# Other layouts for x, the MLP's units and the weight loads of a two-layer decode kernel

## The chip, the core and the metric

The kernel runs on one core of a Trainium2 chip (trn2). The metric is the device time of one execution in microseconds. The kernel before took 519.84, 520.56 and 521.16 us in three runs: a median of 520.56. One more execution was profiled; every duration below that is not called a median comes from it.

## The reference

One token passes through two identical layers. Each layer is an attention block A and an MLP block B, with a residual around each:

```
x = A_x                                         # [1, 1, 640]
twice:
    x = x + A(layernorm(x))
    x = x + B(layernorm(x))

A(x):  q = x @ wq                               # 640 -> 32 heads of 192
       scores of q against the last 4096 keys of each head's cache, softmax, times the values
       return heads @ wo                        # 6144 -> 640
B(x):  h  = gelu(layernorm(x) @ w1)             # shifted along a sequence of length 1:
       x1 = x + 0                               # the shifts push all of h out
       return x1 + gelu(layernorm(x1) @ w3) @ w4   # 640 -> 1536 -> 640
```

Both layers use the same cache and the same weights. All inputs are bf16. Each head's K and V window is 4096 x 192, 1536 KB each.

## The kernel before

**What is kept where.** x is held as a column tile [128, 5]: 640 = 5 x 128. Element `n*128 + p` sits in partition p, column n. The MLP's 1536 units are held as [128, 12]. wq stays in SBUF for the whole kernel (`wq_sb`). A tile `wx_sb` holds the ends of w3 and w4, so that layer 1 reads only the parts that go into cells. Eleven cells of 12 KB a partition take everything else: K and V of one head each, a chunk of wo, w3, w4, transposed K kept from layer 0 for layer 1 (seven heads).

**The order of the loads.** `stream` is a list of all loads, written out by hand: wq and x first, then K and V of the heads with chunks of wo between them, then w3 and w4, and the same for layer 1. SP issues them in this order, up to eight in flight; `take` gives a load the cell that was freed longest ago, so that a load can wait for a cell. Every load is spread over 128 partitions and so over the sixteen DMA engines, eight partitions an engine; a run of contiguous bytes in a partition is a packet.

**Attention** works on groups of four heads. DVE transposes K (L377), PE multiplies it by the spread query (L453), softmax runs across PE, DVE and ACT (L478 to L537), and PE multiplies the probabilities by V (L569). DVE's L576 and PE's L583 fold the result into a column `oT`. A group's part of the product with wo goes one of two ways: `out_proj` (L597) loads a 128x128 block of wo as weights and moves one column through it, 30 blocks a group; `out_row` (L615) loads `oT` as the weights and moves wo's rows through, 2 x 320 columns for each of six chunks, into two rows of an accumulator that `turn_row` (L637) turns into a column afterwards. `out_row` serves four or five middle groups of a layer, `out_proj` the others.

**The mixer** (block B) takes the centred x as `xc`, multiplies it by w3 in 60 blocks of 128x128 (L901, into two halves of six columns each), computes gelu on ACT and DVE (L907 to L920), and multiplies by w4 in 60 blocks (L933). L938 (layer 1) or L940 (layer 0) adds the residual. In layer 0 the next layer's attention follows: mean (L325), q (L407), spread query (L421 to L436), scores. The cells of w3 and w4 are free for the next K and V after L901 and L933.

**Two places where the layout shows.** The unit that w3's block `fc` computes must be the unit that w4's block `fc` expects. w4 is read in pairs of rows (2560 B a run), so w3's columns are taken with a step of two:

```
f0 = 2 * P * (fc // 2) + fc % 2
... lhsT=w3[kc][:, f0:f0 + 2 * P - 1:2], rhs=xc[:, kc:kc + 1]
... y2_ps[:, n:n + 1], lhsT=w4[fc][:, n * P:(n + 1) * P], rhs=hT[:, fc:fc + 1]
```

And x is read as five rows of 128 (L127), cast to f32 (L313) and transposed on PE (L316); the result is transposed back on PE (L954), copied by DVE (L956) and stored as five rows of 256 B (L957).

**Loads in packets.** wq: five loads of 12288 B a partition. w3 in layer 0: two loads, five packets of 3072 B a partition; in layer 1: two loads of two such packets. w4 in layer 0: four loads, five packets of 2560 B and two of 1280; in layer 1: three loads, four of 2560 and one of 1280.

Of the kernel before, what the change touches and what calls it, by code (L numbers as in the profile page):

```python
# [9 lines left out]
F32 = mybir.dt.float32  # L10
# [7 lines left out]
P = 128  # L18
# [17 lines left out]
def kernel(  # L36
# [14 lines left out]
    nc = tc.nc  # L51
# [30 lines left out]
    assert NA * D + FREE - 2 * VW <= FREE  # L82

    W3C, W4C = FREE // F, FREE // D
    assert W4C % 2 == 1 and W4C < NF
# [38 lines left out]
    def load_x():  # L124

        x_bf = wx_sb[0:ND, 4 * P:5 * P]
        nc.sync.dma_start(x_bf, A_x.rearrange("a b (n p) -> (a b n) p", p=P))  # L127
        return x_bf
# [27 lines left out]

    def load_wq(layer, kc):
        nc.sync.dma_start(wq_sb[:, kc, :], A_wq[kc * P:(kc + 1) * P, :])
        return wq_sb
# [192 lines left out]
    def row_space(layer):  # L352

        t, i = ((wx_sb, 8 * P), (kx, 0))[layer]
        return t[0:33, i:i + D].bitcast(F32), t[0:33, i + D:i + D + QC // 2]

    kept = {}
    area = [None, 0]
# [23 lines left out]
    def qproj_steps(c, xc, part=None, row=None):  # L382
# [6 lines left out]
        def project():  # L389
            need("wq", 0, ND - 1)  # L390
            if row is not None:
# [199 lines left out]
    def out_proj(layer, *terms):  # L591

        y_ps = psm.tile([P, ND], F32, tag="psm")
        order = [(c, oT, n, k) for c, oT in terms for k in range(NA) for n in range(ND)]
        for i, (c, oT, n, k) in enumerate(order):
            wo_t = need("wo", layer, c)
            nc.tensor.matmul(  # L597
                y_ps[:, n:n + 1], lhsT=wo_t[:, k * D + n * P:k * D + (n + 1) * P], rhs=oT[:, k:k + 1],
                start=(i == 0), stop=(i == len(order) - 1))
        for c, _ in terms:  # L600
            if (layer, c) == (0, 0):
                loaded["wo", 1, 0] = wo_t
                cell_of["wo", 1, 0] = cell_of.pop(("wo", 0, 0))
            else:
                give(("wo", layer, c))
        return y_ps

    def out_row(layer, c, oT, acc, first):

        wo_t = need("wo", layer, c)  # L610
        N = D // 2
        yr_ps = psm.tile([33, N], F32, tag="psm")
        for k in range(NA):
            for i in range(2):
                nc.tensor.matmul(yr_ps[32 * i:32 * i + 1, :], lhsT=oT[:, k:k + 1],  # L615
                                 rhs=wo_t[:, k * D + i * N:k * D + (i + 1) * N], start=(k == 0), stop=(k == NA - 1))
        give(("wo", layer, c))

        def add():
            for i in range(2):  # L620
                r = slice(32 * i, 32 * i + 1)
                if first:
                    nc.vector.tensor_copy(acc[r, :], yr_ps[r, :])
                else:
                    nc.vector.tensor_add(acc[r, :], acc[r, :], yr_ps[r, :])

        return add

    def turn_row(acc):
        y_ps = psm.tile([P, ND], F32, tag="psm")  # L630
        N = D // 2
        for n in range(ND):
            a, b = n * P, (n + 1) * P
            for i in range(2):
                lo_, hi = max(a, i * N), min(b, (i + 1) * N)
                if lo_ < hi:
                    nc.tensor.matmul(y_ps[lo_ - a:hi - a, n:n + 1], lhsT=acc[:, lo_ - i * N:hi - i * N],  # L637
                                     rhs=ident[0:33, 32 * i:32 * i + 1], start=True, stop=True)
        return y_ps
# [220 lines left out]
    def mixer(layer, x_cur, z, rs_cur, ss_cur, x_new, rs_new):  # L860
# [33 lines left out]
        for ks in kcs:  # L894
            for half, hp in enumerate(h_ps):
                order = ([(i, kc) for kc in ks for i in range(HF)] if ks is kcs[0] else
                         [(i, kc) for i in range(HF) for kc in ks])
                for j, (i, kc) in enumerate(order):
                    fc = half * HF + i
                    f0 = 2 * P * (fc // 2) + fc % 2  # L900
                    nc.tensor.matmul(  # L901
                        hp[:, i:i + 1], lhsT=w3[kc][:, f0:f0 + 2 * P - 1:2], rhs=xc[:, kc:kc + 1],
                        start=(ks is kcs[0] and j == 0), stop=(ks is kcs[-1] and j == len(order) - 1))
# [28 lines left out]
        for i, (n, fc) in enumerate(order):  # L932
            nc.tensor.matmul(  # L933
                y2_ps[:, n:n + 1], lhsT=w4[fc][:, n * P:(n + 1) * P], rhs=hT[:, fc:fc + 1],
                start=(i == 0), stop=(i == len(order) - 1))
# [16 lines left out]

    row_ps = psm.tile([ND, P], out.dtype, tag="psm")
    nc.tensor.transpose(row_ps[:, :], x4[:, :], Eq[:].rearrange("p j b -> p (j b)"))  # L954
    o_fin = Lb[0:ND, :]
    nc.vector.tensor_copy(o_fin, row_ps[:])  # L956
    nc.sync.dma_start(out.rearrange("a b (n p) -> (a b n) p", p=P), o_fin)  # L957

# [29 lines left out]
```

## Time and profile before

| what | value |
|---|---|
| median of three runs | 520.56 us |
| profiled execution: its time | 519.84 us |
| profiled execution: its span | 518.0 us |
| granted TensorE clock, mean | 0.70 |
| PE, DVE, ACT busy | 63%, 57%, 10% |
| bytes read | 216.47 MB, 418 GB/s over the span |
| chain that ended last | DMA 50%, PE 23%, DVE 22% |

The page cuts the span into 40 slices of 13 us. It also has the time of the DMA packets as a share of sixteen engines' span: one queue, SP's, has nearly all of it. The time from issue to landing (part 6 of the page) tells how deep the queue is: 26.3 us for a K load whose bytes take under 4 us to move. Where that is short, 6.2 us for the first load of wq and 7.4 for the shortest V load, little was queued ahead. The chain that ended last is followed back from the last instruction; a DMA piece on it means that the next step waited for that landing, from its issue on. The trace also has every packet, with its size and duration, and for every load one landing mark from each DMA engine; a load has landed with the last of its marks.

PE's group durations are those of one matmul from start to end. Matmuls are pipelined, so where many follow each other their starts tell the pace: for L901 and L933 27 ns from one to the next.

### The profile page before, as it was taken

What the parts mean: (1) busy time and instruction counts of PE and PEld (TensorE: products, weight loads), DVE (VectorE), ACT (ScalarE), POOL (GpSimd) and SP (SyncE); (2) the same over time, 40 slices, a digit from 0 to 9 for tenths busy, and PEclk for the clock granted to TensorE, in tenths of its full rate; (3) what the DMA queues carried; (4) which work ended last, traced back from release to release, by engine and by line L of the source; (5) the groups of instructions that cost most, each with busy time, mean ns of one, the idle gap of its engine ahead of it and who ended that gap; (6) DMA issues with size and microseconds to landing.
All of it is one profiled execution on the core that took longest, in us unless ns stands there. A gap on an engine that the chain in (4) does not pass through costs nothing.

```text
span 518.0 us, 9589 instructions
## 1 busy us (share of the span) xinstructions
PE 324.8 (63%) x4146; PEld 192.6 (37%) x4146; DVE 295.2 (57%) x589; ACT 49.5 (10%) x175; POOL 4.0 (1%) x16
## 2 busy tenths in 40 slices
PE   2057656666664566767755866777566856648665
PEld 2024334333332334434333634434333433425334
DVE  2067667575584655656624356567675765664722
ACT  1000101010010100001011111001010101001011
POOL 2000000000000000000000000000000000000000
PEclk9999878565586755677665778557785676776855
DMA  8999999999999999999999999999999999999995
GB/s 347 433 425 426 433 426 427 432 428 425 433 426 427 431 426 429 428 426 431 424 425 396 385 426 429 428 428 428 429 426 427 432 428 426 426 434 426 427 416 235
DMA packets 23949, 217.08 MB, mean 419 GB/s; under 512 B 2532, under 2 KB 3044, under 8 KB 8420
## 3 DMA queue, kind: packets, MB, share of 16 engines
q1 hardware_dynamic: 23908, 216.48, 99.0%
q8 instruction: 32, 0.52, 0.4%
q14 instruction: 9, 0.07, 0.0%
HBM read 216.47 MB, written 0.00 MB: 418 GB/s over the span
## 4 chain that ended last, share of the span: by engine, by line
DMA 50%; PE 23%; DVE 22%; issue 2%; ACT 1%; SPq 1%; DVEq 0%; ACTq 0%
DMA cell<-in_A_k_cache_dram 39%; DVE cell L377 16%; DMA cell<-in_A_v_cache_dram 9%; PE ST_ps L453 9%; PE O_ps L569 7%; DVE o_sb L576 2%; DMA cell<-in_B_w_dram 2%; DVE pm L478 1%; PE nb_ps L501 1%; DVE o_sb L512 1%; ACT o_sb L507 1%; PE y_ps L637 1%; PE l_ps L528 1%; PE PT_ps L523 1%; PE qT_ps L407 1%
## 5 line engine op out<-in xcount | busy, mean ns | idle before, releaser
L453 PE MATMUL ST_ps<-cell,Qblk 128*16 128x256 bf16 x1536 | 163.7, 380 | 106.9 <-DVE cell L377 69.4
L377 DVE STREAM_TRANSPOSE cell<-cell 128x768 uint32<-128x768 uint32 x228 | 204.1, 945 | 15.2 <-DMA cell<-in_A_k_cache_dram 14.9
L453 PEld LDWEIGHTS <-Qblk 128*16 128x16 bf16 x1536 | 86.1, 111 | 176.5 <-issue 150.3
L569 PE MATMUL O_ps<-cell,PT 128*2 128x384 bf16 x1018 | 99.9, 461 | 8.2 <-DMA cell<-in_A_v_cache_dram 7.4
L576 DVE STREAM_TRANSPOSE o_sb<-O_ps 128x384 f32<-128x384 f32 x64 | 37.2, 581 | 111.8 <-PE O_ps L569 111.6
L569 PEld LDWEIGHTS <-PT 128*2 128x2 bf16 x1024 | 46.0, 100 | 22.1 <-issue 10.1
L512 DVE STREAM_TRANSPOSE o_sb<-o_sb 128x256 bf16<-128x256 bf16 x16 | 7.1, 446 | 33.2 <-ACT o_sb L507 24.2
L584 ACT ACTIVATE oT<-oT_ps,rl 32x6 bf16<-32x6 f32 x40 | 10.3, 258 | 164.0 <-PE oT_ps L583 157.8
L583 PEld LDWEIGHTS oT_ps<-o_sb,Lq 128*32 128x32 f32 x160 | 13.3, 145 | 19.3 <-issue 15.8
L583 PE MATMUL oT_ps<-o_sb,Lq 128*32 128x6 f32 x160 | 13.9, 195 | 10.4 <-DVE o_sb L576 9.9
L589 ACT ACTIVATE oT<-oT_ps,rl 32x6 bf16<-32x6 f32 x24 | 6.2, 258 | 107.6 <-PE ST_ps L453 87.1
L407 PE MATMUL qT_ps<-xc,wq_sb 128*128 128x1 bf16 x210 | 7.1, 165 | 12.8 <-DMA wq_sb<-in_A_wq_dram 12.0
L523 PE MATMUL PT_ps<-o_sb,Eq 128*32 128x32 bf16 x256 | 7.3, 237 | 9.3 <-DVE o_sb L512 4.1
L523 PEld LDWEIGHTS <-Eq 128*32 128x32 bf16 x256 | 5.4, 108 | 19.8 <-issue 19.7
L421 DVE TENSOR_TENSOR Xq<-qT_ps,maskq 128x24 bf16<-128x24 f32 (+1 forms) x18 | 2.8, 158 | 17.1 <-PE qT_ps L407 17.1
L396 PE MATMUL qr_ps<-wq_sb,xc 128*1 128x384 bf16 x90 | 12.1, 415 | 0.0
L407 PEld LDWEIGHTS <-wq_sb 128*128 128x128 bf16 x210 | 6.7, 102 | 14.0 <-DMA wq_sb<-in_A_wq_dram 13.0
L504 ACT COPY nb_sb<-nb_ps 128x1 f32<-128x1 f32 x16 | 2.5, 159 | 94.6 <-PE nb_ps L501 94.6
L615 PE MATMUL yr_ps<-cell,oT 128*1 128x320 bf16 x108 | 11.2, 355 | 0.0
L528 PE MATMUL l_ps<-lh,ones 128*128 128x4 f32 x32 | 7.7, 310 | 4.9 <-ACT PT L526 4.9
L428 PE MATMUL Qrep_ps<-Xq,Lb 128*128 128x24 bf16 (+1 forms) x18 | 3.2, 178 | 11.1 <-DVE Xq L421 10.8
L588 PE MATMUL oT_ps<-o,Lq 128*32 128x6 f32 x48 | 6.1, 199 | 6.5 <-DVE o L587 6.5
(143 smaller groups left out, 200.9 us busy)
## 6 DMA issues: line engine op xcount, KB each, us to landing
cell<-in_A_k_cache_dram SPq DMA_DIRECT2D x57, 1536.0 KB, 26.3
cell<-in_A_v_cache_dram SPq DMA_DIRECT2D x57, 1536.0 KB, 25.8
cell<-in_A_wo_dram SPq DMA_DIRECT2D x13, 960.0 KB, 26.5
wq_sb<-in_A_wq_dram SPq DMA_DIRECT2D x5, 1536.0 KB, 12.2
cell<-in_A_v_cache_dram SPq DMA_DIRECT2D x4, 768.0 KB, 23.8
cell<-in_A_v_cache_dram SPq DMA_DIRECT2D x2, 1248.0 KB, 11.5
cell<-in_B_w_dram SPq DMA_DIRECT2D x1, 1536.0 KB, 11.9
cell<-in_B_w_dram SPq DMA_DIRECT2D x2, 768.0 KB, 10.3
```

Source lines behind the costliest of these rows:

```text
L377: nc.vector.transpose(Tu, Ku[:, :, q * NY:(q + 1) * NY])
L396: nc.tensor.matmul(qr_ps[32 * i:32 * i + 1, :], lhsT=xc[:, kc:kc + 1], rhs=wq_sb[:, kc, t0 * P + i * N:t0 * P + (i + 1) * N], start=(kc == ...
L407: nc.tensor.matmul(qT_ps[:, tl:tl + 1], lhsT=wq_sb[:, kc, t * P:(t + 1) * P], rhs=xc[:, kc:kc + 1], start=(kc == 0), stop=(kc == ND - 1))
L453: nc.tensor.matmul(ST_ps[r:r + QW, :].rearrange("p (g i) -> p g i", g=ng), lhsT=Q[:, n, :], rhs=T4[:, :, f, :, t], start=(hq == 0 and n == ...
L512: nc.vector.transpose(held["PrT"], held["Pr"])
L523: nc.tensor.matmul(PT_ps[32 * m:32 * (m + 1), :, :, ng * q:ng * (q + 1)], lhsT=Eq[:, q, :], rhs=src[:, m:QW:NM], start=True, stop=True)
L528: nc.tensor.matmul(l_ps[:], lhsT=ones[:], rhs=held["lh"][:], start=True, stop=True)
L569: nc.tensor.matmul(O_ps[r:r + 2, :], lhsT=PT[:, hq, 2 * i:2 * i + 2], rhs=v_pair(V, h, 2 * i * Dh, 2 * Dh), start=(i < 4), stop=(i >= NB - 4))
L576: nc.vector.transpose(o_sb[:], O_ps.rearrange("p (e a c) -> p e c a", e=2, c=NA))
L583: nc.tensor.matmul(oT_ps[r, :], lhsT=Lq[:], rhs=o_sb[:, e, :, e], start=(e == 0), stop=(e == 1))
L584: nc.scalar.activation(oT[r, :], oT_ps[r, :], ACTF.Copy, scale=rl[r, 0:1])
L615: nc.tensor.matmul(yr_ps[32 * i:32 * i + 1, :], lhsT=oT[:, k:k + 1], rhs=wo_t[:, k * D + i * N:k * D + (i + 1) * N], start=(k == 0), stop= ...
```

## The change

x goes 5 elements to a partition: element `5*p + n` sits in partition p, column n. The MLP's units go 12 to a partition. So rows 5p to 5p+4 of wq and w3, and rows 12p to 12p+11 of w4, belong to partition p, and lie next to each other in memory.

- wq is read in two loads of 24576 and 36864 B a partition, one packet each.
- w3 is read as one packet of 12288 B (layer 0: and one of 3072 B; layer 1: two of 6144 B). w4: 11520 and 3840 B in layer 0, and 5120, 5120 and 1280 B in layer 1.
- The blocks of weights are read in steps: w3's columns with a step of 12 elements (24 B, before 2 elements), w4's and wo's with a step of 5 (10 B, before 1).
- `out_row` moves wo in steps of 5, 384 columns into one row and 256 into the other; `turn_row` takes five blocks of 128 from them.
- x is read as one row of 1280 B and spread by five matmuls with one row of weights each; the cast and the transpose go.
- The result is stored from the [128, 5] tile, 10 B a partition; the transpose and the copy before the store go.

```diff
+    WQ_PARTS = (0, 2), (2, ND)
...
-        x_bf = wx_sb[0:ND, 4 * P:5 * P]
-        nc.sync.dma_start(x_bf, A_x.rearrange("a b (n p) -> (a b n) p", p=P))
+        x_bf = wx_sb[0:1, 2 * P:2 * P + D]
+        nc.sync.dma_start(x_bf, A_x.rearrange("a b d -> (a b) d"))
...
-    def load_wq(layer, kc):
-        nc.sync.dma_start(wq_sb[:, kc, :], A_wq[kc * P:(kc + 1) * P, :])
+    def load_wq(layer, i):
+        a, b = WQ_PARTS[i]
+        nc.sync.dma_start(wq_sb[:, a:b, :].rearrange("p c n -> p (c n)"),
+                          A_wq.rearrange("(p c) n -> p (c n)", c=ND)[:, a * HD:b * HD])
...
-        src = B_w3.rearrange("(k p) f -> p k f", p=P)
+        src = B_w3.rearrange("(p k) f -> p (k f)", k=ND)
         n = W3C if layer == 0 else W3C // 2
         for k in range(0, W3C, n):
-            nc.sync.dma_start(t[:, k * F:(k + n) * F].rearrange("p (k f) -> p k f", f=F), src[:, k:k + n, :])
+            nc.sync.dma_start(t[:, k * F:(k + n) * F], src[:, k * F:(k + n) * F])
         if layer == 0:
-            nc.sync.dma_start(wx_sb[:, 0:(ND - W3C) * F].rearrange("p (k f) -> p k f", f=F), src[:, W3C:, :])
+            nc.sync.dma_start(wx_sb[:, 0:(ND - W3C) * F], src[:, W3C * F:])
...
-        pairs = B_w4.rearrange("(k p two) n -> p k (two n)", p=P, two=2)
-        ones_ = B_w4.rearrange("(k p two) n -> p k two n", p=P, two=2)
-        h = W4C // 2
-        n = h if layer == 0 else h // 2
-        for k in range(0, h, n):
-            nc.sync.dma_start(t[:, 2 * k * D:2 * (k + n) * D].rearrange("p (k n) -> p k n", k=n), pairs[:, k:k + n, :])
-        nc.sync.dma_start(blocks[2 * h], ones_[:, h, 0, :])
+        src = B_w4.rearrange("(p k) n -> p (k n)", k=NF)
+        h = W4C - 1
+        cuts = [0, W4C] if layer == 0 else [0, h // 2, h, W4C]
+        for a, b in zip(cuts, cuts[1:]):
+            nc.sync.dma_start(t[:, a * D:b * D], src[:, a * D:b * D])
         if layer == 0:
-            nc.sync.dma_start(blocks[2 * h + 1], ones_[:, h, 1, :])
-            rest = NF // 2 - h - 1
-            nc.sync.dma_start(wx_sb[:, x0 + D:x0 + D + 2 * rest * D].rearrange("p (k n) -> p k n", k=rest),
-                              pairs[:, h + 1:, :])
+            nc.sync.dma_start(wx_sb[:, x0:x0 + (NF - W4C) * D], src[:, W4C * D:])
...
-    stream = [("wq", 0, 0), ("x",)] + [("wq", 0, kc) for kc in range(1, ND)] + layer_stream(0) + layer_stream(1)
+    stream = [("wq", 0, 0), ("x",), ("wq", 0, 1)] + layer_stream(0) + layer_stream(1)
...
-    x_rf = wx_sb[0:ND, 6 * P:8 * P].bitcast(F32)
-    nc.vector.tensor_copy(x_rf, x_bf)
...
-    nc.tensor.transpose(xT_ps[:, :], x_rf, ident[0:ND, 0:ND])
+    for n in range(ND):
+        nc.tensor.matmul(xT_ps[:, n:n + 1], lhsT=x_bf[:, n::ND], rhs=Eq[0:1, 0, 0:1], start=True, stop=True)
...
-                y_ps[:, n:n + 1], lhsT=wo_t[:, k * D + n * P:k * D + (n + 1) * P], rhs=oT[:, k:k + 1],
+                y_ps[:, n:n + 1], lhsT=wo_t[:, k * D + n:(k + 1) * D:ND], rhs=oT[:, k:k + 1],
...
+    NR = (ND + 1) // 2
+    ROWS = list(range(NR)), list(range(NR, ND))
...
-            for i in range(2):
-                nc.tensor.matmul(yr_ps[32 * i:32 * i + 1, :], lhsT=oT[:, k:k + 1],
-                                 rhs=wo_t[:, k * D + i * N:k * D + (i + 1) * N], start=(k == 0), stop=(k == NA - 1))
+            w = wo_t[:, k * D:(k + 1) * D].rearrange("q (p n) -> q n p", n=ND)
+            for i, ns in enumerate(ROWS):
+                nc.tensor.matmul(yr_ps[32 * i:32 * i + 1, 0:len(ns) * P].rearrange("o (n p) -> o n p", p=P),
+                                 lhsT=oT[:, k:k + 1], rhs=w[:, ns[0]:ns[-1] + 1, :],
+                                 start=(k == 0), stop=(k == NA - 1))
...
-                        hp[:, i:i + 1], lhsT=w3[kc][:, f0:f0 + 2 * P - 1:2], rhs=xc[:, kc:kc + 1],
+                        hp[:, i:i + 1], lhsT=w3[kc][:, fc::NF], rhs=xc[:, kc:kc + 1],
...
-                y2_ps[:, n:n + 1], lhsT=w4[fc][:, n * P:(n + 1) * P], rhs=hT[:, fc:fc + 1],
+                y2_ps[:, n:n + 1], lhsT=w4[fc][:, n::ND], rhs=hT[:, fc:fc + 1],
...
-    row_ps = psm.tile([ND, P], out.dtype, tag="psm")
-    nc.tensor.transpose(row_ps[:, :], x4[:, :], Eq[:].rearrange("p j b -> p (j b)"))
-    o_fin = Lb[0:ND, :]
-    nc.vector.tensor_copy(o_fin, row_ps[:])
-    nc.sync.dma_start(out.rearrange("a b (n p) -> (a b n) p", p=P), o_fin)
+    nc.sync.dma_start(out.rearrange("a b (p c) -> (a b p) c", c=ND), x4[:])
```

More of the change, by code (lines that the diff above doesn't have):

```diff
@@ L354, in row_space @@
         t, i = ((wx_sb, 8 * P), (kx, 0))[layer]
-        return t[0:33, i:i + D].bitcast(F32), t[0:33, i + D:i + D + QC // 2]
+        n = 2 * NR * P
+        return t[0:33, i:i + n].bitcast(F32), t[0:33, i + n:i + n + QC // 2]
+    NR = (ND + 1) // 2
+    ROWS = list(range(NR)), list(range(NR, ND))
     kept = {}
@@ L389, in project @@
         def project():
-            need("wq", 0, ND - 1)
+            need("wq", 0, len(WQ_PARTS) - 1)
             if row is not None:
@@ L610, in out_row @@
         wo_t = need("wo", layer, c)
-        N = D // 2
-        yr_ps = psm.tile([33, N], F32, tag="psm")
+        yr_ps = psm.tile([33, NR * P], F32, tag="psm")
         for k in range(NA):
-            for i in range(2):
-                nc.tensor.matmul(yr_ps[32 * i:32 * i + 1, :], lhsT=oT[:, k:k + 1],
-                                 rhs=wo_t[:, k * D + i * N:k * D + (i + 1) * N], start=(k == 0), stop=(k == NA - 1))
+            w = wo_t[:, k * D:(k + 1) * D].rearrange("q (p n) -> q n p", n=ND)
[3 more added lines that the diff above has]
+                                 start=(k == 0), stop=(k == NA - 1))
         give(("wo", layer, c))
         def add():
-            for i in range(2):
-                r = slice(32 * i, 32 * i + 1)
+            for i, ns in enumerate(ROWS):
+                r, w = slice(32 * i, 32 * i + 1), slice(0, len(ns) * P)
                 if first:
-                    nc.vector.tensor_copy(acc[r, :], yr_ps[r, :])
+                    nc.vector.tensor_copy(acc[r, w], yr_ps[r, w])
                 else:
-                    nc.vector.tensor_add(acc[r, :], acc[r, :], yr_ps[r, :])
+                    nc.vector.tensor_add(acc[r, w], acc[r, w], yr_ps[r, w])
         return add
@@ L630, in turn_row @@
         y_ps = psm.tile([P, ND], F32, tag="psm")
[L631 to L638, printed above, removed]
+        for i, ns in enumerate(ROWS):
+            for j, n in enumerate(ns):
+                nc.tensor.matmul(y_ps[:, n:n + 1], lhsT=acc[:, j * P:(j + 1) * P],
+                                 rhs=ident[0:33, 32 * i:32 * i + 1], start=True, stop=True)
         return y_ps
@@ L899, in mixer @@
                     fc = half * HF + i
-                    f0 = 2 * P * (fc // 2) + fc % 2
                     nc.tensor.matmul(
-                        hp[:, i:i + 1], lhsT=w3[kc][:, f0:f0 + 2 * P - 1:2], rhs=xc[:, kc:kc + 1],
+                        hp[:, i:i + 1], lhsT=w3[kc][:, fc::NF], rhs=xc[:, kc:kc + 1],
                         start=(ks is kcs[0] and j == 0), stop=(ks is kcs[-1] and j == len(order) - 1))
```

## The prediction

> **What bounds the kernel now.** I read the page's slices first, then the DMA queues, then the chain that ended last in two stretches, then single lines.
>
> ```profile
> DMA  8999999999999999999999999999999999999995
> q1 hardware_dynamic: 23908, 216.48, 99.0%
> ```
>
> The sixteen DMA engines work from the first slice to the last but one. The kernel is a stream of 216 MB, so an edit counts if it shortens the stream, if it starves the stream, or if it lies behind the stream's end. The windows view (busy time of PE, PEld, DVE, ACT, POOL, then clock, DMA share, GB/s) shows where the stream is thin:
>
> ```profile
> 275.00:280.00 5.00, 1.98 (x24) 0.99 (x25) 0.85 (x2) 0.40 (x2) 0.00 (x0) 0.50 1.01 410
> 280.00:285.00 5.00, 3.55 (x94) 3.42 (x94) 1.78 (x15) 1.64 (x8) 0.00 (x0) 0.50 0.97 360
> 291.00:294.00 3.00, 3.00 (x71) 1.99 (x71) 0.36 (x2) 0.46 (x2) 0.00 (x0) 0.77 1.01 366
> 294.00:297.00 3.00, 2.65 (x90) 2.09 (x90) 1.83 (x5) 0.00 (x0) 0.00 (x0) 1.00 0.91 348
> ```
>
> Away from the two ends the page's other slices have 424 to 434 GB/s. These rows are the boundary of the layers, where w3 and w4 of layer 0 are read and where the next loads wait for cells that the mixer frees. The chain there (start, us, what):
>
> ```profile
> 280.17 0.95 PE y_ps L597 x30
> 282.38 0.64 PE V_ps L901 x24
> 283.02 0.64 PE O_ps L901 x24
> 283.66 0.17 PE V_ps L901 x6
> 285.29 1.85 PE y_ps L933 x60
> 290.96 0.12 PE Qrep_ps L428
> ```
>
> It runs from the landing of the last V of layer 0 (277.02) through exactly the matmuls whose weights get a new stride; the K load issued at 291.01 follows the last row. The chain of the end:
>
> ```profile
> 500.70 10.35 DMA cell<-in_B_w_dram
> 511.10 0.50 PE V_ps L901 x12
> 513.94 1.22 PE y_ps L933 x40
> 515.18 0.17 DVE x L938
> 515.40 0.28 PE row_ps L954
> 515.71 0.21 DVE Lb L956
> ```
>
> The second half of w3 lands at 511.05; from there to the store's issue at 515.95 everything is serial.
>
> **The change part by part.** The profiled execution took 519.84 us (span 518.03); the median of the runs is 520.56, so 0.72 is added at the end.
>
> *Packets of the loads.* The trace's packet records give one duration per size: 55 ns for 1280 B, 102 for 2560, 121 for 3072, 460 for 12288. From 3072 to 12288 B that is 0.0368 ns a byte, and every line leaves 8 to 9 ns over: a packet costs 8.5 ns besides its bytes; a completion mark of 4 B costs 9. A DMA engine serves 8 of 128 partitions. wq: 5 x 8 = 40 packets an engine become 16, and three marks go: 24 x 8.5 + 27 = 0.23 us. Layer 0's w3 and w4: 40 + 56 = 96 become 32, two marks go: 0.56 us. Layer 1's w3: 32 become 16: 0.14 us; its w4, 40 to 24, lands at 514.68 while its last block is read near 515.0, so this 0.14 counts nothing. Runs of 24 and 36 KB are not in the queue now; I take the same line for them.
>
> *What of it reaches the end.* Sixteen engines run at different heights: the last half of w3 is finished by the first engine at 507.38, by the last at 511.05, and the landing is the last one's. An engine that never waits keeps 0.23 + 0.56 + 0.14 = 0.93. At the boundary the early engines wait for the K load of 291.01; for them the time is set by the chain above, which starts at a V landing that moved by wq's 0.23 alone: they keep 0.23 + 0.14 = 0.37. Which kind of engine is last at the end the trace does not say; I take the middle, -0.65.
>
> *Strided weights.* w3's columns go from a step of 4 B to 24 B, wo's and w4's from 2 B to 10 B. Nearest rows: L901 (step 4 B) and L933 (2 B) both start a matmul every 27 ns, so a step of 4 B costs nothing. L523, the one bf16 operand read in larger steps (256 B, the moving one), starts every 15 to 16 ns, and its median of 240 ns stands beside 188 for L310, with as many columns read packed: up to 52 ns for 32 columns, in latency, none of it in the pace. Bounds for a strided load: 0, or 27 ns more (the pace halved). I take 0, because L523's pace is the nearest row. At 27 ns: layer 0's chain has 30 (L597) + 54 (L901) + 60 (L933) = 144 loads on it, 3.9 us; the tail has 12 before the first activation (0.32) and 40 of w4 (1.08). L597's slower loads in layer 1 are covered by the 0.89 us for which L901 waits for the DMA before 511.1; w4's first 20, for the most part, by the wait for hT.
> [...]
>
> *out_row and turn_row.* Two matmuls of 320 columns become 384 and 256, in steps of 10 B. The pairs run side by side (starts 3 ns apart, pairs 134 apart): a pair would take 161 ns: 6 x 27 = 0.16 us a call on PE, or 6 x 188 = 1.1 if the pace halves; PV's matmuls queue behind. I cost it at nothing: loads there take 26 us from issue to landing (page, part 6), some seven loads deep, and that depth is the cover; without it nine calls would cost 1.4 to 10 us. turn_row goes from 12 matmul rows to 10, at its 250 to 350 ns: nothing, under the same cover.
>
> *x and start.* x is issued second and queues behind the first part of wq. It landed at 6.9; behind twice the bytes, 3.65 us later, at 10.5. The cast L313 (0.22) and the transpose L316 (0.24) give way to five small matmuls (5 x 27). mean, xc and two DVE memsets behind them come 3.7 us later and are needed at 21.6, when the rest of wq lands: 7 us of cover. q's matmuls of the first columns lose their early start: 4 x 27 = 0.1 us before the first K is turned (25.2), covered too. Fewer, longer loads let SP issue further ahead; nothing waits for that.
>
> *Tail.* L954 and L956 with their two handovers go: from the end of L938 (515.34) to the issue (515.95) is 0.61; a handover to SP of 0.03 to 0.1 stays: -0.55.
>
> *Store.* 5 packets of 256 B become 128 of 10 B, eight on an engine. The trace has packets of 4 B at 9 ns and of 256 B at 15 to 18: 8 x 9 - 15 = +0.06 us on the queue. From the issue to the last mark it takes 1.2 us now, and only this bounds what small writes could cost: as much again. I take +0.2, near the lower row; the bounds are 0 and 1.2. All of it is on the path.
> [...]
>
> **Sum:** -0.65 - 0.55 + 0.2 = -1.0: 518.84 for the profiled execution, **519.6** as a median. What is late next is again w3's last landing and the gelu behind it.
>
> **Rivals.**
> *w3's loads at half pace only.* Layer 0's chain: 54 x 27 = 1.46 late, less 0.23: +1.23 for the K load. The early engines began that load at 293.74 (landing 297.40 less 3.66) and move by +1.23, to 294.97; the last engine came to it at 295.47 and moves by -0.5: middle +0.37; with w3's -0.14, tail -0.55 + 0.32, store +0.2: +0.2, so 520.8. For it: the step of 24 B is the largest of the change. Against it: L523.
> *All strided loads at half pace, slower.* One mechanism, PE's weight reads at the boundary and in the tail: K load 3.9 - 0.23 late, to 297.4 on every engine: the early ones move by +3.7, the last by +1.9, middle +2.8; tail -0.55 + 0.32 + 1.08; store +0.2; w3 -0.14: +3.7, so 524.3. It decides from about 16 ns more a load: middle +1.2, the rest +0.34, past 0.3%. For it: two chains are made of these loads. Against it: L901 against L933.
> *No saving in the stream.* If longer runs cost what they save, tail and store stay: -0.35, so 520.2.
> *More saving.* The last engine at the end is one that never waited (0.93) and the store costs nothing; some of the lag between engines falls away too: -1.5 to -2.2, so 518.7.
>
> **How the numbers follow.** Forecast 0.50, w3 alone 0.15, all loads 0.16, no saving 0.06, more saving 0.13. The runs of before spread over 1.3 us, so 0.3% (1.56 us: under 519.0, over 522.1) is about what a measurement of this kernel can tell from no change. Faster: more saving 0.13 and 0.15 of the forecast, whose lower edge is -1.5: 0.28. Slower: all loads 0.16, and 0.05 of w3 alone and of a store near its upper bound: 0.21. Same: 0.51. The range, 518.2 to 522.0, leaves out all loads at half pace and the edge of more saving. Forecast's own range: 518.8 to 520.4.
>
> **What would show it.** Packets of 24576 and 36864 B near 910 and 1360 ns; 120 packets fewer on each engine; starts of L901's and L933's successors still 27 ns apart (54 proves a rival); the K load behind the boundary at 290.8 and not at 292 to 295; w3's last landing 6.6 us before the end of the span (now 518.03 - 511.05 = 6.98); the store issued 0.05 to 0.1 after L938. The prediction is wrong if the stream between the boundaries changes its pace, or if the store's last mark comes over 1.4 us after its issue.

## The result, and the profile after

The changed kernel took **525.07 us** in the median of six runs (524.64 to 526.0), the kernel before 520.74 beside it on the same chip (519.77 to 521.41): a ratio of 1.0087, 95% interval 1.0072 to 1.0101. That is 4.5 us slower, and outside the range of the prediction. The profiled execution took 525.1 us, its span 523.3, 5.25 more than before's; what follows compares these two executions unless a median is named.

The page's slices and queue, in the changed kernel:

```profile
GB/s 376 410 431 424 428 429 429 431 428 428 426 429 428 430 428 428 430 425 430 427 423 335 390 419 430 428 426 431 427 425 431 428 430 428 427 430 429 423 419 123
DMA packets 22075, 217.08 MB, mean 415 GB/s; under 512 B 2577, under 2 KB 2834, under 8 KB 6674
q1 hardware_dynamic: 22034, 216.48, 97.9%
```

The bytes are the same and the packets are fewer (23908 on q1 before), but the queue's share of the span fell from 99.0% to 97.9%. The lost time sits in one place, the slice with 335 GB/s (396 in the same slice before), and at the end. So neither the longer runs nor the other layout of x seems to hurt; something starves the stream at the boundary of the layers. The windows view of that stretch (columns as in the prediction) finds where; the first row is the kernel before, the others the changed one:

```profile
285.00:288.00 3.00, 2.42 (x62) 2.32 (x63) 1.25 (x10) 0.69 (x3) 0.00 (x0) 0.50 0.95 394
280.00:285.00 5.00, 4.74 (x80) 4.65 (x79) 1.13 (x11) 0.80 (x4) 0.00 (x0) 0.50 0.83 346
285.00:288.00 3.00, 1.88 (x40) 1.83 (x40) 1.63 (x11) 1.41 (x6) 0.00 (x0) 0.50 0.58 184
```

From 285 to 288 us the kernel before moved 394 GB/s, at a DMA share of 0.95; now it is 184, at 0.58. Those 210 GB/s for 3 us are 0.63 MB, 1.5 us of stream at 424 GB/s. Ahead of it PE is busy for 4.74 of 5 us (3.55 before), with fewer instructions. The timeline shows with what (start us, us, engine, line, operation, count, and the idle time before):

```profile
279.86 1.32 PE L597 MATMUL y_ps<-oT,cell 128*128 128x1 bf16 x30 [0.35 <-ACT oT L584]
282.32 1.57 PE L897 MATMUL V_ps<-xc,cell 128*128 128x1 bf16 x24
283.75 1.53 PE L897 MATMUL O_ps<-xc,cell 128*128 128x1 bf16 x24
```

and SP's timeline which loads waited for it (the first two rows are the kernel before):

```profile
283.69 3.39 SPq L145 DMA_DIRECT2D cell<-in_A_v_cache_dram  x2
291.01 2.94 SPq L132 DMA_DIRECT2D cell<-in_A_k_cache_dram  x2
285.31 4.07 SPq L146 DMA_DIRECT2D cell<-in_A_v_cache_dram  x2
293.50 0.33 SPq L133 DMA_DIRECT2D cell<-in_A_k_cache_dram  x1
```

L597's 30 matmuls took 0.95 us before and take 1.32; 24 of w3 (L901 before, L897 now) took 0.64 and take 1.53 to 1.57. Start to start, that is 40 ns a matmul for L597 and w4's L929, and 58 to 60 for w3's L897, where all three lines had 26 to 27 here. The V load into w3's cell, issued at 283.69 before, is issued at 285.31, and the K load at 293.50 instead of 291.01.

The end of the chain that ended last, in the changed kernel:

```profile
509.51 0.78 PE y_ps L597 x15
510.32 0.18 DVE z L687 x2
...
511.56 1.14 PE V_ps L897 x18
512.70 1.08 PE O_ps L897 x18
513.78 0.77 PE V_ps L897 x12
...
516.00 2.63 PE y_ps L929 x60
```

Before, this stretch began with a DMA piece, w3's landing. Now no DMA piece is on it. PE still multiplies w3 when its second half has landed (513.60), and w4's 60 matmuls run without a gap; 60 at 27 ns would be 1.6 us. Behind it stands the store (the last row is the one of the kernel before):

```profile
518.66 0.16 DVE L934 TENSOR_TENSOR x<-base,y_ps 128x5 bf16<-128x5 f32 x1 [1.66 <-PE y_ps L929]
518.85 0.35 SPq L949 DMA_DIRECT2D out_dram<-x  x1
515.95 0.30 SPq L957 DMA_DIRECT2D out_dram<-Lb  x1
```

It is issued straight after the addition, as predicted. Its last mark comes at 522.28, 3.43 us later; in the kernel before it was 515.95 to 517.14, 1.19 us.

The span's 5.25 us, from mark to mark (before, then after):

| stretch | before | after | difference |
|---|---|---|---|
| start to the last V's landing, slowest engine | 502.55 | 505.17 | +2.62 (mean of the 16 marks: +1.77) |
| to z, the end of attention | 5.15 | 5.15 | 0 |
| z to the end of the last addition | 7.64 | 8.50 | +0.86 |
| to the end of the span, with the store | 2.69 | 4.48 | +1.79 |

The slowest engine hangs 1.95 us behind the mean before and 2.80 after; in e1 below it is 1.13, in e6 1.62. It varies with the execution (over all runs 1.1 to 2.4 with the weights as before or packed, 1.5 to 3.1 with steps of 10 or 24 B), so for shares of the cause I use the mean of the marks. The 32 packets of 16384 B in the instruction queue, about 0.93 us each, may be what holds one engine back; no run tests it.

### The profile page after: what moved, and what is told of

Same layout as the page of the kernel before. It is cut to its first block, busy times and chain, and to the rows that moved or that the text cites. A ratio compares the mean times of both kernels' runs of the same rounds, so it can differ in the third digit from the quotient of the medians.

```text
span 523.3 us, 9579 instructions
## 1 busy us (share of the span) xinstructions
PE 341.8 (65%) x4145; PEld 202.3 (39%) x4145; DVE 293.7 (56%) x587; ACT 49.4 (9%) x175; POOL 4.1 (1%) x16
## 3 DMA queue, kind: packets, MB, share of 16 engines
q1 hardware_dynamic: 22034, 216.48, 97.9%
## 5 line engine op out<-in xcount | busy, mean ns | idle before, releaser
L453 PE MATMUL ST_ps<-cell,Qblk 128*16 128x256 bf16 x1536 | 159.0, 369 | 103.7 <-DVE cell L377 70.4
L377 DVE STREAM_TRANSPOSE cell<-cell 128x768 uint32<-128x768 uint32 x228 | 203.8, 943 | 7.4 <-DMA cell<-in_A_k_cache_dram 7.2
L453 PEld LDWEIGHTS <-Qblk 128*16 128x16 bf16 x1536 | 83.5, 109 | 172.6 <-issue 147.2
L569 PE MATMUL O_ps<-cell,PT 128*2 128x384 bf16 x1018 | 101.8, 465 | 9.0 <-DMA cell<-in_A_v_cache_dram 8.3
L569 PEld LDWEIGHTS <-PT 128*2 128x2 bf16 x1024 | 47.1, 101 | 22.9 <-issue 11.3
L615 PE MATMUL yr_ps<-cell,oT 128*1 128x384 bf16 (+1 forms) x108 | 24.4, 530 | 0.0
L407 PE MATMUL qT_ps<-xc,wq_sb 128*128 128x1 bf16 x210 | 6.7, 165 | 10.2 <-DMA wq_sb<-in_A_wq_dram 9.3
L396 PE MATMUL qr_ps<-wq_sb,xc 128*1 128x384 bf16 x90 | 13.2, 446 | 0.0
L523 PE MATMUL PT_ps<-o_sb,Eq 128*32 128x32 bf16 x256 | 7.2, 237 | 8.8 <-DVE o_sb L512 3.5
L615 PEld LDWEIGHTS <-oT 128*1 128x1 bf16 x108 | 8.3, 103 | 10.6 <-issue 9.1
L523 PEld LDWEIGHTS <-Eq 128*32 128x32 bf16 x256 | 5.4, 109 | 14.2 <-issue 14.0
L501 PEld LDWEIGHTS nb_ps<-ones,o_sb 1*128 1x128 f32 x32 | 7.5, 290 | 7.4 <-issue 5.5
```

The lines of the kernel that those rows point to most:

```text
L377: nc.vector.transpose(Tu, Ku[:, :, q * NY:(q + 1) * NY])
L396: nc.tensor.matmul(qr_ps[32 * i:32 * i + 1, :], lhsT=xc[:, kc:kc + 1], rhs=wq_sb[:, kc, t0 * P + i * N:t0 * P + (i + 1) * N], start=(kc == ...
L407: nc.tensor.matmul(qT_ps[:, tl:tl + 1], lhsT=wq_sb[:, kc, t * P:(t + 1) * P], rhs=xc[:, kc:kc + 1], start=(kc == 0), stop=(kc == ND - 1))
L453: nc.tensor.matmul(ST_ps[r:r + QW, :].rearrange("p (g i) -> p g i", g=ng), lhsT=Q[:, n, :], rhs=T4[:, :, f, :, t], start=(hq == 0 and n == ...
L501: nc.tensor.matmul(nb_ps[:], lhsT=held["w"], rhs=ones[0:1, 0:1], start=True, stop=True)
L523: nc.tensor.matmul(PT_ps[32 * m:32 * (m + 1), :, :, ng * q:ng * (q + 1)], lhsT=Eq[:, q, :], rhs=src[:, m:QW:NM], start=True, stop=True)
```

## The experiments

**Theory 1 (the profile's reading):** the weights' steps cost most of the 4.5 us, at the boundary and in the tail, the 10 B store the rest. **Rivals:** the longer runs or the deeper queue disturb the stream; the engines' unequal progress is what grew; `out_row` has a share. The first three runs pack the weights, the store, and both.

**e1_packed** reads w3, w4 and wo's weights packed again. The units then have another order than the loads, so another product is computed.

```diff
-  lhsT=wo_t[:, k * D + n:(k + 1) * D:ND]      +  lhsT=wo_t[:, k * D + n * P:k * D + (n + 1) * P]
-  lhsT=w3[kc][:, fc::NF]                      +  lhsT=w3[kc][:, fc * P:(fc + 1) * P]
-  lhsT=w4[fc][:, n::ND]                       +  lhsT=w4[fc][:, n * P:(n + 1) * P]
```

> The kernel after, but w3, w4 and wo (in out_proj) are read as weights in packed columns, so the units and outputs come in another order and the result is not the reference's. Theory 'two costs' (weight loads in steps make the mixer's chains longer; the store of 10 B runs lands late): the paces go back to 27 ns, the K load behind the boundary is issued 2.9 us earlier (near 290.6), the last V lands where the boundary puts it (near 502), the tail loses 0.86 us: 521.4, against 525.07. Rival 'lag' (the longer runs themselves let the DMA engines drift apart, 4.8 us between first and last at the end against 3.7): only the 1.3 us at the boundary and 0.86 in the tail come back, the drift stays near 4.8: 522.9. Rival 'store alone': 525.

Measured: 521.85 us (520.3 to 522.38), ratio 1.0026 (1.0018 to 1.0035). The profiled execution is the fastest of them, 520.3. All three lines are back at 27 ns, and so are the loads behind the boundary:

```profile
283.35 3.39 SPq L146 DMA_DIRECT2D cell<-in_A_v_cache_dram  x2
290.66 3.19 SPq L133 DMA_DIRECT2D cell<-in_A_k_cache_dram  x2
```

The K load is 0.35 us earlier than in the kernel before, and the last V's marks 0.30 earlier in the mean. Against the changed kernel the ratios differ by 0.0061, 3.2 us (some 2.3 to 4.1 by the two intervals). This is the weights' price. What is left over the kernel before, 1.0026, is not told apart from what the store costs by itself (1.0020 in e5 below, either with some 0.0009 to each side), so the medians show no price and no gain of the loads' layout.

**e2_rowstore** is the changed kernel with the result turned into one row and stored as one run of 1280 B; **e3_both** does the same with the weights packed.

```diff
-    nc.sync.dma_start(out.rearrange("a b (p c) -> (a b p) c", c=ND), x4[:])
+    for i, ns in enumerate(ROWS):
...
+            nc.tensor.transpose(r_ps[0:1, j * P:(j + 1) * P], x4[:, n:n + 1], Eq[:].rearrange("p j b -> p (j b)"))
+        nc.vector.tensor_copy(o_row.rearrange("o (p n) -> o n p", n=ND)[:, ns[0]:ns[-1] + 1, :], ...)
+    nc.sync.dma_start(out.rearrange("a b d -> (a b) d"), o_row)
```

> The kernel after, but the result is first turned into one row (five transposes on PE, two copies on DVE) and stored as a single run of 1280 B. Theory 'two costs': from the store's issue to its last mark 1.2 us instead of 3.4, the turn costs 0.9: 523.8. Rival 'store alone' (all of the loss is at the end): 521. Rival 'the store is not it' (the late marks are the normal end of any store after a 128 partition tile): 526.

> Both edits of the two kernels before at once (columns packed, so the result is not the reference's; stored as one row). Theory 'two costs': the two gains add, 525.07 - 3.7 - 1.3 = 520.1, at or a little under the kernel before. Rival 'lag': 521.6.

Measured: e2 527.08 (ratio 1.0121, 1.0106 to 1.0136) and e3 522.32 (1.0035, 1.0022 to 1.0048). Both missed. The store itself did what was expected: issue to last mark 1.13 us. The turn did not: the two copies that write one partition in steps of 10 B are far slower than I had them. The chain of e2:

```profile
518.63 0.17 DVE x L934
518.84 0.49 PE r_ps L953 x3
519.36 1.21 DVE wx_sb L954
520.57 0.71 DVEq L982
```

The issue comes at 521.30, 2.5 us after the addition, and takes back the 2.3 us that the store gained. That makes e2 as slow as the changed kernel, and its profiled execution, 525.21, is; but it is the fastest of e2's five (525.21 to 527.64). In the median e2 is 0.0034, or 1.8 us, slower than the changed kernel, and what the others lose there stays open.

**e4_steps_weights** measures the disputed cost by itself: 16 equal matmuls of one column for each of ten steps of the weights, on wq's tile while nothing else runs on PE (one execution, as with e9 and e10 below).

```diff
+   for i in range(16): nc.tensor.matmul(sw_ps[:], lhsT=wq_sb[:, 0, 0:127 * s + 1:s], rhs=Eq[:, 0, 0:1], ...)   # s = 1, 2, 3, ... 32
```

> The kernel after, with 16 matmuls for each of ten steps of the weights' columns (2, 4, 6, 8, 10, 12, 16, 24, 32 and 64 B) put where PE waits for the second part of wq; their results are not used. [...]

Three of the ten lines (min, median, max ns of one; first and last start in us), steps of 2, 10 and 24 B:

```profile
L644 PE MATMUL sw_ps<-Eq,wq_sb x16: 165/165/166, 11.4 to 11.8; 128*128 128x1 bf16 x16
L648 PE MATMUL sw_ps<-Eq,wq_sb x16: 177/178/178, 13.2 to 13.8; 128*128 128x1 bf16 x16
L651 PE MATMUL sw_ps<-Eq,wq_sb x16: 196/197/198, 15.6 to 16.5; 128*128 128x1 bf16 x16
```

The duration hardly moves, 165 to 197 ns; the pace is in the starts. From the records, start to start, with those of **e10_steps_moving** beside them (five equal matmuls of 256 moving columns for each step, weights packed):

```diff
+   for i in range(5): nc.tensor.matmul(sw_ps[:], lhsT=Eq[:, 0, :], rhs=wq_sb[:, 0, 0:255 * s + 1:s], ...)   # s = 1, 2, 4, 5, 6, 8, 12, 16
```

| step in bytes | 2 | 4 | 6 | 8 | 10 | 12 | 16 | 24 | 32 | 64 |
|---|---|---|---|---|---|---|---|---|---|---|
| a load of 128x128 weights, ns | 26.7 | 26.7 | 28.3 | 32.8 | 39.9 | 46.6 | 61.1 | 58.5 | 61.6 | 59.3 |
| 256 moving columns, ns | 213 | 213 | | 227 | 283 | 340 | 451 | 449 | 460 | |

> The kernel after with five matmuls of 256 moving columns for each of eight steps (2, 4, 8, 10, 12, 16, 24, 32 B), put where PE waits for wq; results not used. [...] Rival 'the moving side is free', as L523 seemed to say: 107 ns at every step.

Measured: the two curves have one shape. Against the packed pace of these two runs (26.7 and 213 ns), a step of 4 B is free (the same two numbers), steps of 16 B and more cost a factor of 2.1 to 2.3, up to the largest measured (64 B for weights, 32 B for moving columns), and 10 B lies between, 1.5 for weights and 1.33 for moving columns. Below that, 6 B costs 1.6 ns a load, and 8 B 6 ns a load and 14 ns on the 256 columns. e10's 107 ns for the packed columns missed: they took 213.

The 107 came from `out_row` in the kernel before, whose pairs start 134 ns apart for 320 columns. That is its pace at a granted clock of 1.00. In its calls at 0.50 the pairs are 267 apart, 0.83 ns a column, and that is also e10's packed pace. The windows view gives a clock of 1.00 there, but no clock record lies ahead of 14.6 us in e10, nor ahead of 35.2 in e4. One call of `out_row` shows what the clock does (busy time of L615 and of its weight loads, clock, DMA share, GB/s; two rows of the kernel before, then two of the changed one):

```profile
81.00:84.00 3.00, 0.98 (x12) 0.52 (x12) 1.00 1.07 452
207.00:210.00 3.00, 1.76 (x12) 0.59 (x12) 0.50 0.99 422
81.00:85.00 4.00, 2.70 (x12) 0.91 (x12) 1.00 1.03 434
207.00:211.00 4.00, 2.70 (x12) 0.82 (x12) 0.50 1.02 431
```

The packed pace of moving columns follows the clock (134 ns a pair at 1.00, 267 at 0.50); the pace in steps of 10 B doesn't (2.70 us a call at both). So the factor depends on the clock: 353 ns a pair in e13 below against 267 is 1.3 at 0.50, and against 134 it is 2.6 at 1.00. For weights it matters little: L597 starts every 25 ns at 1.00 and 27 at 0.50 when packed, and every 40 at both in steps of 10 B. Steps of 24 B in w3 ran at 0.50 alone, at 58 to 60 ns.

**e5_before_store10, e6_before_steps, e7_w3_packed, e8_out_row_packed** put single parts into the kernel before, or take them out of the changed one. e5: before, with the direct 10 B store (a permuted result). e6: before, with the steps of w3, w4 and wo's weights and nothing else (other products). e7 and e8: the changed kernel with w3 alone, or `out_row`'s moving columns alone, packed (other products).

```diff
e5  -    nc.tensor.transpose(row_ps[:, :], x4[:, :], ...)   # and the copy
    +    nc.sync.dma_start(out.rearrange("a b (p c) -> (a b p) c", c=ND), x4[:])
e6  +    lhsT=wo_t[:, k * D + n:(k + 1) * D:ND] ... lhsT=w3[kc][:, fc::NF] ... lhsT=w4[fc][:, n::ND]
e7  +    lhsT=w3[kc][:, fc * P:(fc + 1) * P]
e8  +    rhs=wo_t[:, k * D + ns[0] * P:k * D + (ns[-1] + 1) * P].rearrange("q (n p) -> q n p", p=P)
```

> The kernel before, but its [128, 5] result is stored directly as 128 runs of 10 B, without the turn and the copy; its elements land in the change's order, so the result is not the reference's. Theory 'two costs': the issue comes 0.58 us earlier, the last mark 3.1 to 3.4 us after it instead of 1.2: +1.6, so 522.1 for a kernel before at 520.5. Rival 'only after late loads' (the marks came late in the kernel after because w4's last transfers were still moving): -0.5.

> The kernel before with the change's steps of the weight columns alone (24 B for w3, 10 B for w4 and wo's out_proj), on before's loads, so units and outputs are mixed and the result is not the reference's. Theory 'two costs': K load behind the boundary 2.9 us later (293.9), the mean over the engines' marks there +1.4, of the last w3 +1.7, tail +0.86: +2.6 to +3.0, so 523.3. Rival 'lag' (the longer runs let the engines drift): +2.2 at most. Rival 'steps are covered': 520.5.

> The kernel after with w3 alone read in packed columns (other units, so the result is not the reference's); wo and w4 keep their 10 B step. Theory: of the 2.9 us at the boundary 54 x 32 ns = 1.7 go, of the tail 0.33; of the time 1.0 (boundary, in the mean over the engines) + 0.33: 523.7 for a kernel after at 525.1. If the loss were w4's and wo's alone: 525.0.

> The kernel after, but out_row moves wo's rows in packed columns (outputs mixed, so the result is not the reference's). A pair of its matmuls falls from 275 to about 161 ns, 0.7 us a call. Theory: covered by the depth of the stream, the time stays within 0.3 us of the kernel after. Rival: the nine calls delay PE's chain, -1 to -2 us.

| kernel | median us | ratio to before (interval) |
|---|---|---|
| e5_before_store10 | 521.05 | 1.0020 (1.0010 to 1.0029) |
| e6_before_steps | 523.61 | 1.0066 (1.0052 to 1.0081) |
| e7_w3_packed | 523.53 | 1.0067 (1.0054 to 1.0079) |
| e8_out_row_packed | 524.03 | 1.0074 (1.0059 to 1.0089) |

e5 gains 0.60 us by its earlier issue (515.35) and loses 1.60 by the mark (2.79 us after the issue): +1.0, which is the store edit's whole price, and the median says the same (1.6 was expected: the mark was forecast 3.1 to 3.4 us after the issue). e6 shows that the steps alone, without a byte or a packet moved, cost 3.4 us, as e1 had it from the other side; the rival that the longer runs disturb the stream falls; it allowed 2.2 at most here. e6's profiled execution is its slowest, 524.75. Its window from 285 to 288 us:

```profile
285.00:288.00 3.00, 1.89 (x38) 1.84 (x37) 1.22 (x9) 1.17 (x5) 0.00 (x0) 0.50 0.60 161
```

is the changed kernel's hole again. e7 is some 1.0 us better than the changed kernel by the ratios (1.3 was expected), barely clear of zero by the two intervals; its V load behind w3 is issued at 283.96 instead of 285.31. e8's 0.7 us lies within the two intervals and settles nothing.

**e9_store_shapes** stores the same 1280 B in six shapes, one after the other, each waiting for the last, before the real store.

```diff
+    nc.sync.dma_start(out.rearrange("a b (p c) -> (a b p) c", c=5), wx_sb[0:128, 0:5])   # then c=10, 20, 40, 128, 640
```

> The kernel after with six more stores of 1280 B each in front of the last one, one waiting for the other, after the result is there: 128 runs of 10 B, 64 of 20, 32 of 40, 16 of 80, 5 of 256, 1 of 1280 (they write other values, the true store comes last; the time is longer by their sum). Theory 'short runs': issue to last mark about 3.3 us for 10 B, falling with the length of the run, 1.2 for 256 and 1280 B. Rival 'sixteen engines': all that use sixteen engines (10 to 80 B) take 3 us alike, 256 and 1280 B 1.2.

The first of the six, the last of them, and the real store:

```profile
519.33 0.35 SPq L951 DMA_DIRECT2D out_dram<-wx_sb  x1
528.39 0.23 SPq L956 DMA_DIRECT2D out_dram<-wx_sb  x1
529.50 0.36 SPq L957 DMA_DIRECT2D out_dram<-x  x1
```

| packets | 128 x 10 B | 64 x 20 | 32 x 40 | 16 x 80 | 5 x 256 | 1 x 1280 | 128 x 10 again |
|---|---|---|---|---|---|---|---|
| issue to last mark, us | 3.29 | 1.75 | 1.45 | 1.31 | 1.16 | 1.10 | 2.62 |

The price rises with the number of packets (and as their size falls; the total is the same): sixteen cost 0.2 more than a single run, 64 cost 0.65, 128 cost 1.5 to 2.2. The packet records themselves show 7 to 9 ns for each, and in the changed kernel all 128 are done by 519.88; the mark follows up to 2.4 us later. So the time lies between the last packet's record and the mark, which the trace doesn't divide further. The rival 'only after late loads' of e5 falls too: the last store of e9 comes over 13 us after the last load has landed and still takes 2.62. The runs fit a price for each packet written, 10 to 17 ns by the table (5 x 256 B cost 0.06 us more than one run, 12 ns a packet), and don't show what it is made of.

**e11_three_units** tries for a version that is better than both: the kernel before, with three units a partition for w4 (3840 B a run) and a step of 6 B in w3, which e4 has at 28.3 ns.

```diff
-        pairs = B_w4.rearrange("(k p two) n -> p k (two n)", p=P, two=2)
+        src = B_w4.rearrange("(g p j) n -> p g (j n)", p=P, j=3)
...
-                        hp[:, i:i + 1], lhsT=w3[kc][:, f0:f0 + 2 * P - 1:2], rhs=xc[:, kc:kc + 1],
+                        hp[:, i:i + 1], lhsT=w3[kc][:, f0:f0 + 3 * P - 2:3], rhs=xc[:, kc:kc + 1],
```

> The kernel before, with three units of the MLP in a partition instead of two: w4 in runs of 3840 B (three runs in the cell and one in the rest; five and two before), w3's columns with a step of 6 B, and in layer 1 six of w4's blocks ahead of the second half of gelu. Computes the reference. Theory: 24 packets and two marks fewer in layer 0 (0.2 us), 10 matmuls fewer behind the last gelu (0.27), 54 loads of 28 instead of 27 ns (+0.1): -0.4, so about 520.1 for a kernel before at 520.5, hardly clear of it; by a rule that a step of more than 4 B costs: +1.

Measured: 521.03, ratio 1.0013 (1.0003 to 1.0022): a miss. One cause is in its chain: w4's loads of layer 1 are now three equal ones, so the last, which lands at 514.77, has 15 matmuls behind it:

```profile
505.12 9.65 DMA cell<-in_B_w_dram
514.82 0.57 PE y_ps L927 x15
```

Before, a small load came last, and w4's matmuls ended at 515.16; here at 515.39. The rest of the 0.6 us I didn't find. None of the versions is faster than the kernel before.

**e12_no_steps and e13_before_out_row** were for `out_row`. The traces gave a reason to doubt its cover: in layer 1 the transposes of K (L377) run 12 to 17 us behind the landings at first and work that off, to 0.1 us at the K that lands near 431 us in the kernel before and in e8, but only to 3.8 in the changed kernel and 6.0 in e6. e12 is the changed kernel with every read packed; e13 is the kernel before with `out_row`'s columns in steps of 10 B (both compute other products).

```diff
e12  e1's three lines and e8's
e13  +  rhs=wo_t[:, k * D:(k + 1) * D].rearrange("q (h p n) -> q h p n"...)   # as "q h n p", half i: five runs of 64 columns
```

> The changed kernel with every read packed again: w3's, w4's and wo's weights as in the earlier packed version, and out_row's moving columns too, so that units of another order are multiplied and the result is not the reference's; layouts, longer runs, x and the direct store stay. In the traces so far the DVE's transposes of K run behind the landings by 12 to 17 us at the start of layer 1 and work that off; at the K load that lands near 431 us the lag is 0.1 us in the kernel before and in the version with out_row packed, and 2.7 to 6.0 us in every version with out_row in steps. Theory A, out_row's steps eat the engines' catching up and in part of the executions that reaches the end: here the lag near 431 us is under 0.5, and the median is 521.0 to 521.4 (before, plus 1.2 for the store, less 0.3 to 0.6 for the packets), below the 521.85 of the version with the weights alone packed. Theory B, out_row's steps are covered to the end: the lag may vary, the median is as with the weights alone packed, 521.7 to 522.0.

> The kernel before with one edit: out_row's moving columns are read in steps of 10 B (two halves of five runs of 64 columns), so that its result is not the reference's. Theory A: a pair of matmuls starts about 275 ns after the last instead of 134, five calls in layer 1 lose about 0.85 us each, the lag near 431 us is 2.5 to 6 us instead of 0.1, and the median is 0.5 to 1.0 above before. Theory B, as the prediction had it: the lag does not matter, the median is within 0.3 of before.

Measured: e12 521.43, ratio 1.0019 (1.0008 to 1.0031); e13 520.57, 1.0006 (0.9995 to 1.0016). In e13 the group of L615 grew

```profile
L615 PE MATMUL yr_ps<-cell,oT 128*1 128x320 bf16 x108 | 20.6, 531 | 0.0
```

from 11.2 us (mean 355 ns), the pairs 353 ns apart instead of 134 to 267, and the lag near 431 us grew to 3.3 us; and the median moved by 0.3, which is not told apart from nothing. e12 lies between what the two theories gave it, and is 0.0007 under e1, within their intervals. My theory, that the lag has a price, falls as far as `out_row` alone goes. It falls in its mechanism too: e12 reads nothing of wo, w3 or w4 in steps and shows a lag of 3.4 there. What the traces suggest is a threshold at the end. "Lag" is how long after the last K's landing its transposes begin, "to z" how long after that landing attention ends:

| kernel | before | e12 | e13 | changed | e1 | e2 | e9 | e7 | e6 |
|---|---|---|---|---|---|---|---|---|---|
| lag, us | 2.8 | 2.7 | 3.3 | 3.9 | 4.4 | 5.9 | 6.1 | 5.9 | 6.7 |
| to z, us | 27.2 | 27.1 | 27.6 | 27.2 | 27.2 | 28.6 | 28.9 | 30.0 | 29.6 |

e3, e5 and e11 have lags of 2.5 to 3.2 and 27.1 to 27.2 to z, e10 and e4 6.8 and 7.6, with 29.6 and 30.4. So up to 4.4 us the lag is hidden (27.1 to 27.6), and from 5.9 on attention ends 1.4 to 3.2 later; but e8 doesn't fit, with a lag of 3.1 and 28.5 to z. The six executions above the threshold all have steps in weights; e2 and e9 are the changed kernel up to z. So part of the weights' price may reach the end by this way in some executions. How often, what made e8 late, and why the lag differs between executions, stays open.

## Why the prediction was wrong

It forecast 519.6 (518.2 to 522.0), "same" as the likeliest. The rival **All strided loads at half pace, slower** named the mechanism, the place and the sign; its 524.3 had the store at +0.2 and the loads at 27 ns more. That it comes so near 525.07 is in part luck: it had the loads too dear (3.9 us at the boundary, where 2.9 came, and 1.40 in the tail, where 0.86 came) and the store too cheap, and these errors cancel. Step by step:

- **Strided weights: failed, and it decided.** The step said: "Bounds for a strided load: 0, or 27 ns more (the pace halved). I take 0, because L523's pace is the nearest row." Measured: 13 ns more for steps of 10 B and 32 for 24 B, the second a little outside the bounds. By 30 x 13 + 54 x 32 + 60 x 13 the boundary's chain is 2.90 us longer; it starts 0.31 us earlier (last V of layer 0 at 276.71 instead of 277.02), so the K load should move by 2.59, and moved by 2.49. In the median the weights cost 3.2 us (e1) to 3.4 (e6).
- **Why L523 misled.** Its starts are 13.4 to 14.5 ns apart in the mean of a call, at granted clocks of 1.00 and 0.50 alike. At 0.50 a packed column takes 0.83 ns, so 32 take 27 ns, as L310's starts show too; 14 ns is less, so several of L523's matmuls must run at a time, and the code writes to four groups of 32 partitions. If four run side by side, which no run tests by itself, one group's 32 columns take some 56 ns by my estimate (4 x 14.1): 1.8 ns a column, against 0.83 packed (L310 and e10) and 1.76 at a step of 16 B or more in e10. Read so, the row I took for "no cost" already had the halved pace. L901 against L933 was read rightly, but 4 B says nothing of 10 or 24: the curve is flat up to there (26.7 ns at 2 and at 4 B).
- **Store: failed.** "I take +0.2, near the lower row; the bounds are 0 and 1.2." It is +1.6 (e5) and +2.24 in the profiled execution: outside both bounds. "As much again" as 1.2 had no row behind it; the packet records (8 x 9 ns) end up to 2.4 us before the last mark. The sign that the prediction named for this, a mark over 1.4 us after the issue, is there. With the issue's gain the end of the kernel got 1.0 us worse, not 0.35 better.
- **Tail, -0.55: right** in size (0.60 in e5; the issue is at once behind the addition). **Packets: right** as durations: 912 ns for 24576 B and 1364 for 36864, where 910 and 1360 were forecast. (The four lines of the working leave about 8 ns a packet, not 8.5; on 104 packets that is 0.05 us.)
- **What of it reaches the end, -0.65: at its lower bound or below.** With the weights packed, the K load moved by -0.35 in e1, -0.17 in e3 and -0.16 in e12, and the mean of the last V's marks by -0.30, -0.20 and -0.08 (bounds -0.37 and -0.93); in the medians nothing of it can be told, e12's 1.0019 being e5's 1.0020.
- **x and start: right.** x landed at 10.2 (forecast 10.5), and the first K's transposes begin with the landing, as before.
- **out_row and turn_row at nothing: right for the median, with the size wrong and the cover in doubt.** The working read the pairs at a granted clock of 1.00 alone and bounded a call's loss at 1.1 us. A call takes 2.70 us, 1.7 more than before at 1.00 and 0.9 more at 0.50; the nine together take 24.4 us of PE where 11.2 were. (The 275 ns of e8's and e13's texts is the pace of the 256 columns; the 384 beside them start 424 apart.) The depth of the queue is 24 us still, but in layer 1 K's transposes run up to 13.7 us behind the landings, so what hides the loss there is the room to work that lag off. That is argued from the lags; no run tests it.
- **The tail's matmuls.** The +0.86 us between z and the last addition is +0.33 to the first activation, where w3's slower loads stand in place of the 0.89 us that PE waited for w3 before, and +0.53 behind it, 40 x 13 for w4. The prediction's rival had 0.32 and 1.08.

By the ratios the parts, each put alone into the kernel before, add up: the weights' steps 0.0066 (e6), the store 0.0020 (e5), `out_row` 0.0006 (e13): 1.0092, against 1.0087 measured, within the intervals.

## What to carry to other kernels

Longer runs in DRAM that are paid for with steps inside SBUF move the cost from the DMA engines to PE's weight loads, and PE pays each time that it loads them: here the 144 loads of the boundary's chain took 2.90 us longer, where the change with packed weights had the K load 0.35 us earlier (e1). A column of a layout "n units a partition" is a step of 2n bytes in bf16: measured here, 4 B is free (26.7 ns a load, as packed), 10 B costs half as much again (39.9) and 16 to 64 B more than double the load (58.5 to 61.6). Before a pace is taken from a row, look at how many instructions run side by side in it and at which granted clock (`out_row`'s packed pairs took 134 ns at 1.00 and 267 at 0.50); and price a store by its last mark (here 3.43 us after the issue), not by its packets (the last record ends 1.03 us after it).

## What the runs showed of the hardware that was not expected

- The cost of a step is not two-valued: 26.7, 28.3, 32.8, 39.9, 46.6, 61 ns a load for 2 or 4, 6, 8, 10, 12, 16 B, then flat to 64 B (58.5 to 61.6). At 10 B the pace is the same at granted clocks of 1.00 and 0.50: 40 ns a load, 2.70 us a call of `out_row`. Packed, that call takes 0.98 us at 1.00 and 1.76 at 0.50.
- A store of 128 runs of 10 B has its last mark 2.6 to 3.6 us after its issue in all runs that have it, one of 1280 B after 1.1, although each small packet holds its engine for 9 ns only.
- Two DVE copies of 384 and 256 elements into a single partition in steps of 10 B take 1.91 us together (e2), against 0.69 for the five transposes ahead of them; packed copies of as many f32 columns into one partition (L624) take 0.54 and 0.42 in the changed kernel.
